# Two of sixteen hidden blocks of the first group changed from whole fp32 products to split fp32r products, with the instruction order rebuilt

## The chip, the cores and the metric

The kernel runs on one core of one Trainium2 chip. The metric is the device time of one execution in microseconds (us); the figure compared is the median of several runs. The core has five engines that matter here: PE (TensorE, matrix products; PEld is its weight load), DVE (VectorE), ACT (ScalarE), POOL (GpSimd) and SP (SyncE, which only issues DMAs here).

## The reference

Gated linear attention over 4 batches and 8 heads, 768 steps, head size 48, and then a feed-forward layer on its output:

```python
for t in range(S):
    state = alpha[:, :, t, :, None] * state + np.einsum('bhd,bhe->bhde', k[:, :, t], v[:, :, t])
    y[:, :, t] = np.einsum('bhd,bhde->bhe', q[:, :, t], state)
x = y.transpose(0, 2, 1, 3).reshape(3072, 384)
h = x @ w_in                          # w_in 384 x 2048
g = np.where(h >= 1, h, np.where(h <= -1, 0.0, (h + 1) ** 2 / 4))
return (g @ w_out).astype(np.float32) # w_out 2048 x 384
```

The two weight matrices come as float64 and are turned into fp32 on the chip.

## The kernel before

**Attention.** The 3072 tokens are 24 chunks of 128 (6 per batch, the batches in turn). For each chunk `prepare` loads gates, keys, queries and values (1.28 MB) and runs two scans and two products on DVE (L478 to L510); `begin_chunk` turns the keys (a PE transpose for chunks 0 to 6, later a DVE transpose and DMAs); the scores and the state update are short fp32 matmuls on PE (L589, L602). `follow` masks the scores: on DVE by a product with a 0/1 mask (L709, two halves u for each of two head parities r), or, for r = 1 of chunks 0 to 6 (`HELP`), by two ACT copies (L681) and one POOL `affine_select` (L691). Then the outputs of the chunk are computed (L769) and copied to x by `end_chunk`. From chunk 5 on (`MERGE`) the outputs of chunk j-1, the update and the scores of chunk j are one burst on PE; before, they are separate pieces.

**Feed-forward.** Three chunks are a group (8 groups of 384 tokens). A group has 16 blocks of 128 hidden units. `hidden` makes h for one block, then ACT and DVE make g (L918 twice, L928), and `second` adds g times its rows of w_out to three PSUM banks that stay open over the group. In group 0 (`WHOLE = 1`) both products are whole fp32 matmuls (L878, L960), on weights as decoded. In groups 1 to 7 both are split: weight and operand are each a sum of a rounded fp32r part and an fp32r rest, and three fp32r products (part by part, part by rest, rest by part) stand for one fp32 product (L887, L969). This needs a cast on ACT and a subtraction on DVE for g (L937, L938) and for x (L804, L809).

**Weights.** Each of 8 pairs of blocks has two tensors (in and out). A tensor is loaded as float64, decoded by ACT and DVE (L349 to L388, five instructions), and, for the split form, parted by `part_w` into a new buffer: an ACT cast (L394) and then, for pairs 0 to 4 (`BYSUM`), an ACT negation (L397) and an accumulating DMA issued by POOL (L402), or, for pairs 5 to 7, a DVE subtraction (L395). Decoded and parted tensors share one pool of `2 * NU + MORE` = 18 buffers of 6 KB per partition; 16 of them hold the decoded tensors, and a decoded one is free once it is parted and its blocks of group 0 are done.

**Order.** `Plan` gathers every instruction with a cost and a key (a due time, in units of one block) and orders all engines by a list scheduler written in the kernel: on each engine, of the instructions that can start soon, the one with the smallest key goes first. The constants at the top of the file and the table `OFF` shift keys. Where PE would be idle near the start, matmuls on zeros (`fill`, L1020) are put in. The order is fixed when the kernel is built; each engine runs its list in that order and waits on semaphores.

Of the kernel before, what the change touches and what calls it, by code (L numbers as in the profile page):

```python
# [27 lines left out]
WHOLE = 1  # L28
PLACED = (0, 1, 2, 5)
MORE = 2  # L30
NV = 3
WARM = 10
LAG = 4.0
FETCH = 9
LOAD = 12.0
DECODE = 3.5
PARTED = 4.0
PREPARE = 0.5
# [12 lines left out]
HELP = 7  # L51
BYSUM = 5
LATE = 14
TURN = 7
EARLY = 3.0
BYDMA = 24
NEAR = 0.2


OFF = {'b0': 4.6, 'b1': -0.3, 'b2': -25, 'b5': -25, 'b6': 3.7, 'b7': 3.5, 'di0': -6.0, 'di1': 2.6, 'di2': 2.7, 'di4': -0.2, 'di5': -0.8, 'di6': -0.8, 'di7': 2.3, 'do0': 5.0, 'do1': -1.1, 'do2': 0.1, 'do4': -0.1, 'do5': 0.3, 'do6': 0.5, 'fi0': -6.2, 'fi1': -10.5, 'fi2': 1.1, 'fi3': 2.0, 'fi4': 1.4, 'fi5': 0.2, 'fi6': -0.6, 'fi7': 17.6, 'fo0': -15.3, 'fo1': -6.3, 'fo2': 2.4, 'fo3': 1.9, 'fo4': 12.3, 'fo5': 7.6, 'fo6': -8.0, 'fo7': 1.1, 'l0': -6.5, 'l1': 0.1, 'l2': -6.9, 'l3': -2.8, 'l4': 3.7, 'l5': -12.4, 'l7': -0.8, 'l8': 0.3, 'p0': -0.3, 'p1': -0.4, 'p2': 0.2, 'p3': -20.7, 'p4': 1.6, 'p5': 1.3, 'p7': -1.3, 'p8': 1.5, 'q0': 0.1, 'q1': 5.5, 'q2': -22.8, 'q3': 15.7, 'q4': -13.5, 'q5': -8.8, 'q6': -14.1, 'q7': 14.6, 'q8': -14.2, 't1': 2.7, 't2': -24.0, 't3': 0.9, 't4': -1.7, 't5': -8.7, 't6': -8.6, 't8': -8.1, 'v0': 3.6, 'v1': 9.0, 'v2': -6.4, 'v3': 1.8, 'v4': 11.4, 'v5': -8.3, 'v6': -3.5, 'v7': 0.3, 'v8': 9.8, 'wi0': 0.3, 'wi2': -4.3, 'wi3': -19.9, 'wi4': -19.0, 'wi5': -0.7, 'wi6': 4.0, 'wi7': 10.0, 'wo0': -0.7, 'wo2': -6.1, 'wo3': 2.3, 'wo4': 1.4, 'wo5': -3.3, 'wo6': 2.7, 'wo7': 25, 'y1': 0.1, 'y2': 1.0, 'y3': -5.9, 'y4': -1.8, 'y5': -10.9}  # L60
off = lambda *k: OFF.get("".join(map(str, k)), 0.0)

# [179 lines left out]
def gated_attention_ffn(ctx: ExitStack, tc: tile.TileContext, q, k, v, alpha, w_in, w_out, by, out):  # L242
# [61 lines left out]
    with ExitStack() as main:  # L304
# [86 lines left out]
        def part_w(u, which, raw, parts, key):  # L391
            part = lambda a: parts().rearrange(PARTS[which])[:, a * n_w : (a + 1) * n_w]
            data = lambda: whole_w(raw())
            plan.op("ACT", 0.83, key, lambda: nc.scalar.copy(out=part(0), in_=data()), [raw], [parts])  # L394
            sub = lambda e: e.tensor_tensor(out=part(1), in0=data(), in1=part(0).bitcast(F32), op=ALU.subtract)  # L395
            if u < BYSUM:
                plan.op("ACT", 0.86, key, lambda: nc.scalar.mul(out=part(1), in_=part(0).bitcast(F32), mul=-1.0), [parts], [parts])  # L397
                plan.op(
                    "POOL",
                    1.0,  # L400
                    key,
                    lambda: nc.gpsimd.dma_start(out=part(1), in_=data(), accum_op=ALU.add),  # L402
                    [raw, parts],
                    [parts],
                    moved=P * n_w * 4,
                    land=0.8,
                    rate=Plan.SUM,
                )
                return
            plan.op("DVE", 0.95, key, lambda: sub(nc.vector), [raw, parts], [parts], port=True)  # L410
# [245 lines left out]
        def follow(j, key):  # L656
# [17 lines left out]
            for r, to in enumerate((Q, other)):  # L674
                for u in range(2):
                    if r and j < HELP:
                        plan.op(
                            "ACT",
                            0.39,
                            key,  # L680
                            lambda u=u: nc.scalar.copy(out=other()[0:HC, :, halves[u]], in_=ss(j, 1)[halves[u]]),  # L681
                            [meets[j][1]],
                            [other],
                            beside=True,
                        )
                        if u:
                            plan.op(
                                "POOL",
                                0.62,
                                key,  # L690
                                lambda: nc.gpsimd.affine_select(  # L691
                                    out=other()[0:HC].rearrange("p g (u t) -> p g u t", u=2),
                                    in_=other()[0:HC].rearrange("p g (u t) -> p g u t", u=2),
                                    compare_op=ALU.is_ge,
# [4 lines left out]
                                ),  # L699
                                [other],  # L700
                                [other],
                                port=True,
# [54 lines left out]
        whole_x = lambda n: xs[n]()[:, rest_n : rest_n + KT * groups[n] * CH].rearrange("p (k j t) -> p k j t", k=KT, j=groups[n])  # L757
        plan.op("POOL", 0.75, -98.0, lambda: nc.gpsimd.memset(rest_b(), 0.0), [], [xs[0]])

        def outputs(j, ps):  # L760
# [106 lines left out]
        def hidden(n, f, key):  # L867
# [3 lines left out]
            gf = buf("fw", "gf", [P, L], 3)  # L871
            whole = n < WHOLE

            def product():
                m = 0
                for kt in range(KT):
# [9 lines left out]
                    for w, a in ((0, 0), (0, 1), (1, 0)):  # L886
                        nc.tensor.matmul(  # L887
                            out=h(),
                            lhsT=win(f, w)[:, kt],
                            rhs=xs[n]()[:, 0 : groups[n], kt, a],  # L890
                            start=(m == 0),
# [4 lines left out]
            u = f // NW  # L896
            needs = [xs[n], *([*[("x", first[n] + c) for c in range(groups[n])], raws_w[u][0]] if whole else [("moved", n), wi[u]])]

# [50 lines left out]
        def second(seg, f, gh, key):  # L949
# [4 lines left out]

            whole = n < WHOLE

# [66 lines left out]
        for u in range(NU):  # L1023
            weights(u)
        at = 0

        for j in range(NCH):
# [217 lines left out]
```

## Time and profile before

| | |
|---|---|
| median of 3 runs | 501.81 us (501.47 to 501.83) |
| the profiled execution | 501.42 us, of which 499.7 us is the span from its first to its last instruction |
| PE busy | 491.5 us (98% of the span) |
| DVE busy | 347.3 us (69%) |
| ACT busy | 317.9 us (64%) |
| POOL busy | 30.5 us (6%) |
| granted TensorE clock, mean | 0.999 |

The busy times are unions over the span. The shares are averages over stages: DVE and ACT are much busier in the first 150 us than later. A matmul on PE overlaps the next one, so the sum of single durations is more than the busy time; the pace of a run of matmuls is read from the chain, where a piece stands with its own length.

### The profile page before, as it was taken

What the parts mean: (1) busy time and instruction counts of PE and PEld (TensorE: products, weight loads), DVE (VectorE), ACT (ScalarE), POOL (GpSimd) and SP (SyncE); (2) the same over time, 40 slices, a digit from 0 to 9 for tenths busy, and PEclk for the clock granted to TensorE, in tenths of its full rate; (3) what the DMA queues carried; (4) which work ended last, traced back from release to release, by engine and by line L of the source; (5) the groups of instructions that cost most, each with busy time, mean ns of one, the idle gap of its engine ahead of it and who ended that gap; (6) DMA issues with size and microseconds to landing.
All of it is one profiled execution on the core that took longest, in us unless ns stands there. A gap on an engine that the chain in (4) does not pass through costs nothing.

```text
span 499.7 us, 11372 instructions
## 1 busy us (share of the span) xinstructions
PE 491.5 (98%) x4586; PEld 446.5 (89%) x4586; DVE 347.3 (69%) x609; ACT 317.9 (64%) x603; POOL 30.5 (6%) x70
## 2 busy tenths in 40 slices
PE   8899999999999999999999999999999999999996
PEld 3665656699999999999999999999999999999995
DVE  6998999998997866865866857767755635343332
ACT  3799998998765565565665655665565655555551
POOL 4211102211000000000000000000000000000000
PEclk9999999999999999999999999999999999999999
DMA  8999916878552531542434513434313201001001
GB/s 315 394 387 387 330 23 142 208 201 181 181 159 65 187 102 49 150 137 82 110 95 118 174 47 124 130 100 139 115 35 89 70 1 25 1 7 42 0 1 51
DMA packets 43336, 64.42 MB, mean 129 GB/s; under 512 B 21392, under 2 KB 30736, under 8 KB 43280
## 3 DMA queue, kind: packets, MB, share of 16 engines
q1 hardware_dynamic: 41840, 59.71, 37.4%
q0 software_dynamic: 1440, 3.93, 4.2%
q8 instruction: 38, 0.62, 0.5%
q14 instruction: 18, 0.15, 0.1%
HBM read 48.56 MB, written 9.18 MB: 116 GB/s over the span
## 4 chain that ended last, share of the span: by engine, by line
PE 94%; DVE 3%; issue 1%; DMA 1%; POOL 0%; ACT 0%; DVEq 0%
PE ps L969 36%; PE ps L887 35%; PE ps L878 6%; PE ps L960 6%; PE ps L769 5%; PE ps L602 3%; PE ps L589 2%; DVE inv L485 1%; DVE pre L478 1%; DMA raw_a<-in_al 1%; PE ps L574 1%; DVE inv L493 0%; DVE Q L709 0%; DVE Q L510 0%; DVE state L653 0%
## 5 line engine op out<-in xcount | busy, mean ns | idle before, releaser
L969 PE MATMUL ps<-gh,wt 128*128 128x384 f32 x1008 | 197.1, 340 | 0.0
L887 PE MATMUL ps<-xs,wt 128*128 128x384 f32 x1008 | 193.6, 335 | 0.0
L969 PEld LDWEIGHTS ps<-gh,wt 128*128 128x128 f32 x1008 | 177.7, 188 | 1.3 <-issue 0.2
L887 PEld LDWEIGHTS ps<-xs,wt 128*128 128x128 f32 x1008 | 176.7, 188 | 0.7
L928 DVE SCALAR_TENSOR_TENSOR gf<-gf,ps 128x384 f32<-128x384 f32 x128 | 70.6, 552 | 94.0 <-ACT gf L918 92.5
L918 ACT ACTIVATE gf<-ps,half_b 128x384 f32<-128x384 f32 x128 | 74.4, 582 | 83.4 <-PE ps L887 80.5
L937 ACT CAST gh<-gf 128x384 fp32r<-128x384 f32 x112 | 57.4, 513 | 59.0 <-DVE gf L928 49.7
L938 DVE TENSOR_TENSOR gh<-gf,gh 128x384 fp32r<-128x384 f32 x112 | 62.0, 555 | 33.3 <-ACT gh L937 32.6
L918 ACT ACTIVATE gf<-gf 128x384 f32<-128x384 f32 x128 | 67.2, 525 | 4.0
L635 ACT COPY both<-state 48x192 f32<-48x192 f32 x88 | 30.8, 350 | 10.5 <-PE ps L602 9.1
L960 PE MATMUL ps<-gf,wt 128*128 128x384 f32 x96 | 33.0, 488 | 0.4 <-PE ps L878 0.4
L878 PE MATMUL ps<-xs,wt 128*128 128x384 f32 x96 | 32.7, 489 | 0.1
L478 DVE TENSOR_TENSOR_SCAN pre<-raw_a,fwd 128x516 f32<-128x516 f32 x24 | 29.5, 1228 | 3.0 <-DMA raw_a<-in_al 2.7
L485 DVE TENSOR_TENSOR_SCAN inv<-raw_a,bwd 128x516 f32<-128x516 f32 x24 | 30.1, 1254 | 2.1
L769 PEld LDWEIGHTS ps<-Q,both 128*64 128x64 f32 x368 | 23.2, 138 | 7.2 <-issue 5.6
L960 PEld LDWEIGHTS ps<-gf,wt 128*128 128x128 f32 x96 | 18.0, 190 | 12.4 <-PE ps L878 0.8
L878 PEld LDWEIGHTS ps<-xs,wt 128*128 128x128 f32 x96 | 17.8, 190 | 11.9 <-ACT wt L357 0.4
L769 PE MATMUL ps<-Q,both 128*64 128x64 f32 x368 | 26.6, 225 | 0.0
L769 PE MATMUL ps<-other,both 128*64 128x64 f32 x368 | 26.6, 225 | 0.0
L501 POOL COPY meet<-inv 128x4 f32<-128x4 f32 x24 | 9.8, 408 | 258.3 <-DVE inv L485 258.3
L769 PEld LDWEIGHTS ps<-other,both 128*64 128x64 f32 x368 | 23.2, 138 | 0.0
L709 DVE TENSOR_TENSOR Q<-ps,mask 64x256 f32<-64x256 f32 x48 | 20.3, 423 | 3.6 <-ACT other L672 1.8
(62 smaller groups left out, 370.1 us busy)
## 6 DMA issues: line engine op xcount, KB each, us to landing
raw_kq<-in_kq SPq DMA_DIRECT2D x24, 512.0 KB, 5.2
both<-in_vl SPq DMA_DIRECT2D x24, 512.0 KB, 4.6
raw_a<-in_al SPq DMA_DIRECT2D x24, 258.5 KB, 3.3
wt<-in_w_out SPq DMA_DIRECT2D x8, 768.0 KB, 9.4
wt<-in_w_in SPq DMA_DIRECT2D x8, 768.0 KB, 8.4
out<-ot SPq DMA_DIRECT2D x24, 192.0 KB, 3.1
turned<-w SPq DMA_DIRECT2D x17, 256.0 KB, 2.2
ks<-turned SPq DMA_DIRECT2D x68, 64.0 KB, 2.6
```

Source lines behind the costliest of these rows:

```text
L478: lambda: nc.vector.tensor_tensor_scan(flat(pre()), a[:, 0:n], flat(fwd), 0.0, ALU.mult, ALU.max),
L485: lambda: nc.vector.tensor_tensor_scan(flat(inv())[:, ::-1], a[:, 1 : n + 1][:, ::-1], flat(bwd)[:, ::-1], 0.0, ALU.mult, ALU.max),
L635: lambda r=r, to=to: nc.scalar.copy(out=to, in_=state[low[r], b]),
L769: nc.tensor.matmul(out=ps()[halves[r], to, halves[u]], lhsT=lhsT[:, u, r], rhs=x()[:, g, halves[u]], start=m + u == 0, stop=True, skip_gro ...
L878: nc.tensor.matmul(out=h(), lhsT=raw_in(f)[:, kt], rhs=whole_x(n)[:, kt].rearrange("p j t -> p (j t)"), start=kt == 0, stop=kt == KT - 1,)
L887: nc.tensor.matmul(out=h(), lhsT=win(f, w)[:, kt], rhs=xs[n]()[:, 0 : groups[n], kt, a], start=(m == 0), stop=(m == 3 * KT - 1),)
L918: lambda: nc.scalar.activation(out=gf(), in_=in_(), func=func, scale=scale, bias=bias),
L928: lambda: nc.vector.scalar_tensor_tensor(out=gf(), in0=gf(), scalar=1.0, in1=h(), op0=ALU.min, op1=ALU.max),
L937: plan.op("ACT", 0.08 + 0.41 * w, key + 0.4, lambda: nc.scalar.copy(out=gh()[:, 0], in_=gf()), [gf], [gh])
L938: sub = lambda e: e.tensor_tensor(out=gh()[:, 1], in0=gf(), in1=gh()[:, 0].bitcast(F32), op=ALU.subtract)
L960: nc.tensor.matmul(out=o_ps[seg][m](), lhsT=raw_out(f)[:, m * P : (m + 1) * P], rhs=gh(), start=f == f0, stop=f == f1 - 1,)
L969: nc.tensor.matmul(out=o_ps[seg][m](), lhsT=wout(f, w)[:, m * P : (m + 1) * P], rhs=gh()[:, a], start=(f == f0 and i == 0), stop=(f == f1 ...
```

## The change

The last two blocks (14 and 15, one pair) of group 0 are computed in split form (`PLAIN = 14`). For that, a new function `split_x` parts the x of group 0's three chunks into a new tile `xl` (9 KB per partition), pair 7 is parted in the time of group 0 instead of group 1, and g of these two blocks is parted too. To make room, the weight pool goes from 18 to 17 buffers (`MORE`) and the tile `gh` from 3 buffers to 2. For chunks 0 to 2 (`HELP0 = 3`) the masks of r = 0 go from DVE to ACT and POOL as well, and for r = 1 this is done for chunks 0 to 9 (`HELP = 10`) instead of 0 to 6. Bursts begin with chunk 4 instead of 5 (`MERGE`). `BYCAST` is 0, so its branch in `part_w` is never taken. All margins and most of `OFF` are new, so the order is another one.

```diff
-MORE = 2
+MORE = 1
+PLAIN = 14
+SPLIT = 3.5
+HELP0 = 3
+BYCAST = 0
-FETCH = 9
+FETCH = 10
-PARTED = 4.0
+PARTED = 5.0
-MARGIN0 = 18.0
-MARGIN1 = 8.0
+MARGIN0 = 9.0
+MARGIN1 = 6.0
-DECODE0 = 10.0
-AHEAD = 26
-FIRST = 3
+DECODE0 = 7.0
+AHEAD = 30
+FIRST = 4
-LATER = 8
-MERGE = 4
+LATER = 4.5
+MERGE = 3
-SOON = 5.5
-HELP = 7
+SOON = 8
+HELP = 10
-OFF = {'b0': 4.6, ...}
+OFF = {'b1': -0.2, ...}
...
-    step = [groups[n] / 3 * (1.2 if n < WHOLE else 1.0) for n in range(NG)]
+    step = [groups[n] / 3 * (1 + 0.2 * PLAIN / NF if n < WHOLE else 1.0) for n in range(NG)]
...
-            key = begin[WHOLE] + u * NW * step[WHOLE] - PARTED
+            n = 0 if (u + 1) * NW > PLAIN else WHOLE
+            key = begin[n] + u * NW * step[n] - PARTED
...
-                    if r and j < HELP:
+                    if j < (HELP0, HELP)[r]:
...
+        xl = buf("xs", "xl", [P, 2, KT, groups[0] * CH], 1, F32R)
+
+        def split_x(n):
+            key = begin[n] + PLAIN * step[n] - SPLIT
+            for c in range(groups[n]):
+                j = first[n] + c
+                to = lambda a, c=c: xl()[:, a].rearrange("p k (j t) -> p k j t", j=groups[n])[:, :, c]
+                o = plan.op(
+                    "ACT", 0.5, key + off("x", j), lambda c=c, to=to: nc.scalar.copy(out=to(0), in_=whole_x(n)[:, :, c]),
+                    [xs[n], ("x", j)], [xl], beside=c > 0,
+                )
+                plan.op(
+                    "DVE", 0.55, key + off("x", j),
+                    lambda c=c, to=to: nc.vector.tensor_tensor(
+                        out=to(1), in0=whole_x(n)[:, :, c], in1=to(0).bitcast(F32), op=ALU.subtract
+                    ),
+                    [xs[n], ("x", j)], [xl], beside=True, after=[o], port=True,
+                )
...
-            whole = n < WHOLE
+            whole = n < WHOLE and f < PLAIN
+            split = lambda kt, a: xl()[:, a, kt] if n < WHOLE else xs[n]()[:, 0 : groups[n], kt, a]
...
-            gh = buf("fw", "gh", [P, 2, L], 3, F32R)
+            gh = buf("fw", "gh", [P, 2, L], 2, F32R)
...
+        for u in range(NU):
+            parts_of(u)
...
-                if at == WHOLE:
-                    for u in range(NU):
-                        parts_of(u)
+                if at < WHOLE and PLAIN < NF:
+                    split_x(at)
```

## Rows read from the trace of the kernel before

**Rows 1.** Waits of PE: engine, line, waited-for engine and line: us, times, longest.

```profile
PE ps L574 <- DVE inv L493: 1.6, 2, 0.9
PE ps L960 <- PE ps L878: 0.4, 1, 0.4
```

**Rows 2.** Chain that ended last, in order of time: start us, us, what.

```profile
28.53 4.12 PE ps L878 x12
33.09 2.10 PE ps L960 x6
...
71.07 3.87 PE ps L878 x12
74.94 3.87 PE ps L960 x12
...
96.31 2.78 PE ps L960 x8
99.09 3.14 PE ps L887 x18
...
106.64 1.58 PE ps L969 x9
...
166.58 1.59 PE ps L969 x9
...
172.87 1.58 PE ps L969 x9
```

**Rows 3.** Timeline of DVE: start us, us, engine line op tiles [idle before].

```profile
10.48 1.63 DVE L485 TENSOR_TENSOR_SCAN inv<-raw_a,bwd 128x516 f32<-128x516 f32 x1
...
15.55 1.23 DVE L485 TENSOR_TENSOR_SCAN inv<-raw_a,bwd 128x516 f32<-128x516 f32 x1
16.82 0.86 DVE L709 TENSOR_TENSOR Q<-ps,mask 64x256 f32<-64x256 f32 x2
...
27.47 0.96 DVE L388 CUSTOM_DVE_ANT_0 wt<-wt,w 128x1536 uint16<-128x1536 uint16 x1
...
32.23 0.55 DVE L928 SCALAR_TENSOR_TENSOR gf<-gf,ps 128x384 f32<-128x384 f32 x1
...
93.94 0.96 DVE L388 CUSTOM_DVE_ANT_0 wt<-wt,w 128x1536 uint16<-128x1536 uint16 x1
...
169.72 0.53 DVE L938 TENSOR_TENSOR gh<-gf,gh 128x384 fp32r<-128x384 f32 x1
```

**Rows 4.** Timeline of POOL, chunk 0's mask.

```profile
10.37 0.66 POOL L691 TENSOR_SCALAR_AFFINE_SELECT other<-other 64x512 f32<-64x512 f32 x1
```

**Rows 5.** Groups by line and shape: busy us, mean ns of one | idle before.

```profile
L938 DVE TENSOR_TENSOR gh<-gf,gh 128x384 fp32r<-128x384 f32 x112 | 62.0, 555 | 33.3 <-ACT gh L937 32.6
L937 ACT CAST gh<-gf 128x384 fp32r<-128x384 f32 x112 | 57.4, 513 | 59.0 <-DVE gf L928 49.7 <-DVE bwd L482 6.8 <-PE ps L969 2.1
L395 DVE TENSOR_TENSOR wt<-wt 128x768 fp32r<-128x768 f32 x6 | 5.7, 946 | 0.0
L681 ACT COPY other<-ps 64x256 f32<-64x256 f32 x14 | 5.1, 368 | 0.6 <-PE ps L602 0.5
```

**Rows 6.** Busy time by stage: us, PE, PEld, DVE, ACT, POOL, PEclk, DMA, GB/s.

```profile
25.00:50.00 25.00, 24.39 (x208) 15.18 (x207) 23.10 (x33) 22.96 (x36) 2.99 (x5) 1.00 1.01 387
50.00:75.00 25.00, 25.00 (x142) 15.05 (x141) 23.64 (x35) 23.10 (x39) 3.01 (x4) 1.00 0.55 177
75.00:98.00 23.00, 23.00 (x270) 15.07 (x269) 21.02 (x35) 20.72 (x37) 5.32 (x9) 1.00 0.73 169
```

**Rows 7.** Timeline of ACT: a parting cast that waited, and its negation.

```profile
84.15 0.83 ACT L394 CAST wt<-wt 128x768 fp32r<-128x768 f32 x1 [1.05 <-DMA wt<-wt]
85.01 0.84 ACT L397 ACTIVATE wt<-wt 128x768 fp32r<-128x768 f32 x1
```

**Rows 8.** Lines L394 and L402: ns min/median/max, first and last start; time to landing.

```profile
L394 ACT CAST wt<-wt x16: 807/829/838, 42.2 to 134.7; 128x768 fp32r<-128x768 f32 x16
...
DMA to landing us min/median/max: 3.9/6.3/9.8
```

More of the change, by code (lines that the diff above doesn't have):

```diff
@@ L29 @@
 PLACED = (0, 1, 2, 5)
-MORE = 2
+MORE = 1
 NV = 3
+PLAIN = 14
+SPLIT = 3.5
+HELP0 = 3
+BYCAST = 0
 WARM = 10
 LAG = 4.0
-FETCH = 9
-LOAD = 12.0
+FETCH = 10
+LOAD = 12
 DECODE = 3.5
-PARTED = 4.0
-PREPARE = 0.5
+PARTED = 5.0
+PREPARE = 1.0
 MARGIN = 9.0
-MARGIN0 = 18.0
-MARGIN1 = 8.0
+MARGIN0 = 9.0
+MARGIN1 = 6.0
 FETCH0 = 16
-DECODE0 = 10.0
-AHEAD = 26
-FIRST = 3
+DECODE0 = 7.0
+AHEAD = 30
+FIRST = 4
 ROOM = 6
-LATER = 8
-MERGE = 4
+LATER = 4.5
+MERGE = 3
 WARMTH = 40
-SOON = 5.5
-HELP = 7
+SOON = 8
@@ L393, in part_w @@
             data = lambda: whole_w(raw())
-            plan.op("ACT", 0.83, key, lambda: nc.scalar.copy(out=part(0), in_=data()), [raw], [parts])
+            hi = (parts, "hi")
+            if u >= NU - BYCAST:
+                plan.op(
+                    "POOL",
+                    1.0,
+                    key,
+                    lambda: nc.gpsimd.dma_start(out=part(0), in_=data()),
+                    [raw],
+                    [parts, hi],
+                    moved=P * n_w * 4,
+                    land=0.8,
+                    rate=Plan.SUM,
+                )
+                plan.op("ACT", 0.86, key, lambda: nc.scalar.mul(out=part(1), in_=data(), mul=-1.0), [raw], [parts], beside=True)
+                plan.op(
+                    "POOL",
+                    1.0,
+                    key,
+                    lambda: nc.gpsimd.dma_start(out=part(1), in_=data(), accum_op=ALU.add),
+                    [raw, parts],
+                    [parts],
+                    moved=P * n_w * 4,
+                    land=0.8,
+                    rate=Plan.SUM,
+                )
+                return
+            plan.op("ACT", 0.83, key, lambda: nc.scalar.copy(out=part(0), in_=data()), [raw], [parts, hi])
             sub = lambda e: e.tensor_tensor(out=part(1), in0=data(), in1=part(0).bitcast(F32), op=ALU.subtract)
@@ L680, in follow @@
                             key,
[L681 to L684, printed above, removed]
+                            lambda r=r, u=u, to=to: nc.scalar.copy(out=to()[halves[1 - r], :, halves[u]], in_=ss(j, r)[halves[u]]),
+                            [meets[j][r], other],
+                            [to],
+                            beside=r + u > 0,
                         )
+                        masks.append(o)
                         if u:
@@ L690, in follow @@
                                 key,
-                                lambda: nc.gpsimd.affine_select(
-                                    out=other()[0:HC].rearrange("p g (u t) -> p g u t", u=2),
-                                    in_=other()[0:HC].rearrange("p g (u t) -> p g u t", u=2),
+                                lambda r=r, to=to: nc.gpsimd.affine_select(
+                                    out=to()[halves[1 - r]].rearrange("p g (u t) -> p g u t", u=2),
+                                    in_=to()[halves[1 - r]].rearrange("p g (u t) -> p g u t", u=2),
                                     compare_op=ALU.is_ge,
@@ L699, in follow @@
                                 ),
-                                [other],
-                                [other],
+                                [to],
+                                [to],
                                 port=True,
@@ L889, in product @@
                             lhsT=win(f, w)[:, kt],
-                            rhs=xs[n]()[:, 0 : groups[n], kt, a],
+                            rhs=split(kt, a),
                             start=(m == 0),
@@ L896, in hidden @@
             u = f // NW
-            needs = [xs[n], *([*[("x", first[n] + c) for c in range(groups[n])], raws_w[u][0]] if whole else [("moved", n), wi[u]])]
+            if whole:
+                needs = [xs[n], *[("x", first[n] + c) for c in range(groups[n])], raws_w[u][0]]
+            else:
+                needs = [*([xl] if n < WHOLE else [xs[n], ("moved", n)]), wi[u]]
             firsts[:] = [
@@ L953, in second @@
                 o_ps[seg] = [bank("ps_o", KT, [P, L]) for _ in range(KT)]
-            whole = n < WHOLE
+            whole = n < WHOLE and f < PLAIN
             def product(ms):
```

11 lines of the change are left out of this document (7 added, 4 removed).

## The prediction

> **What bounds the kernel now.** I read the waits of PE first. All waits of PE in the whole execution are a few, short, and lie at the start: the largest is 1.6 us on the products that `prepare` makes on DVE, and the latest is 0.4 us before the first second-layer block [rows 1]. From 33 us to the end of the last block PE never waits. So past 33 us the time can fall only by less work on PE, and it can rise by any stall that comes in; before 28.53 us, when the first hidden block starts [rows 2], it is what holds that start.
>
> Next, the chain in order of time, for the pace of PE. Two hidden blocks in whole form are one piece of 3.87 us, so one is 1.935 us, and two second-layer blocks took the same; two hidden blocks in split form are 3.14 us, so one is 1.57 us, and a split second-layer block is 1.58 us [rows 2]. The first piece after attention matmuls is some 0.2 us longer (4.12 against 3.87) [rows 2].
>
> Then the timeline of DVE, for the start. It works almost without a gap from 3.8 us on, through the preparation of chunks 0 to 3, their masks and the decoding of the first weight tensor, whose last instruction ends at 28.43 us, 0.1 us before the first hidden block [rows 2, 3]. So DVE sets the start. The 0.4 us before the first second-layer block is DVE's too: it makes g at 32.23 to 32.78 us and PE goes on at 33.09 us [rows 2, 3].
>
> Last, busy time by stage, for the cover under group 0. Of 73 us from 25 to 98 us, DVE is idle 1.90 + 1.36 + 1.98 = 5.24 us, and ACT 2.04 + 1.90 + 2.28 = 6.22 us [rows 6]. Both engines nearly fill group 0, although PE does not wait for them.
>
> **The change part by part.**
>
> *Two blocks in split form.* Two hidden blocks fall from 3.87 us to 3.14 us and two second-layer blocks from 3.87 us to 3.16 us: 0.73 + 0.71 = 1.44 us less on PE, which is the bound there. Both forms are measured at this size and the granted clock is 1.00 in these stages [rows 6], so this term I take as it stands.
>
> *Masks off DVE at the start (`HELP0`).* For each of chunks 0, 1 and 2, two mask products on DVE, 0.86 us together [rows 3], become two ACT copies of 0.37 us [rows 5] and one POOL select of 0.66 us [rows 4]. That is 3 x 0.86 = 2.6 us off the engine that sets the start. It does not come free: a select on POOL at 10.37 us lies over the scan that starts at 10.48 us, which took 1.63 us where its like took 1.23 us [rows 3, 4], so a select can cost DVE 0.40 us. Taking half of that for each, since a select may also meet an instruction that it leaves alone, the gain is 3 x (0.86 - 0.20) = 2.0 us; the bounds are 0 (if the longer way over ACT and POOL holds chunk 2's x until the old time) and 2.6 us. I take 2.0, because DVE's list and not the latency of a chunk ends just before the first block.
>
> The Trainium skill (SBUF — State Buffer, section Who interferes with whom) says that a DVE instruction with two SBUF inputs and a GpSimd instruction that reads SBUF share a port, and that the loser is blocked for the whole of the other. The 0.40 us that the scan lost agrees in kind, with less than the select's whole 0.66 us. By that rule in full the gain at the start would be 3 x (0.86 - 0.66) = 0.6 us, and the forecast 1.4 us later; it speaks against this part of the change.
>
> *The first wait of the second layer.* Chunk 3 becomes due later than the first block (its margin falls by 2 and its shift rises), so the g of the first block can come ahead of chunk 3's masks on DVE: up to 0.4 us [rows 1]. Bounds 0 and 0.4; I take 0.4.
>
> *Bursts from chunk 4 on.* The separate outputs of chunk 3 join a burst; one change between attention and blocks goes, 0.2 us [rows 2].
>
> *More work on DVE and ACT in group 0.* Parting x: three casts and three subtractions of the size of those of g, 3 x 0.51 us on ACT and 3 x 0.56 us on DVE. Parting g of two blocks: 2 x 0.51 and 2 x 0.56 us. Pair 7 parted there instead of later: 2 x 0.83 on ACT and 2 x 0.95 on DVE [rows 5, 8]. Sum: DVE 1.67 + 1.11 + 1.89 = 4.67 us, ACT 4.2 us. What hides it is the idle time of the two engines, 5.24 and 6.22 us. But group 0 also becomes shorter on PE by 1.44 + 0.2 us; so DVE would need 4.67 + 1.64 = 6.3 us and has 5.24. The lack of 1.1 us, and the 0.4 us of the item before, which only moves PE ahead of the same DVE work, comes back as a wait at the end of group 0 if DVE can't be filled better. That end is tight already: the last decoding of a weight tensor starts at 93.94 us and ends at 94.90 us, and the second-layer blocks that follow in the chain start at 96.31 us [rows 2, 3]; now a parting of some 1.8 us must fit between. Bounds 0 (the work of chunks 6 and 7 is put off) and 1.5 us. Behind a late second-layer block 14 stand block 15 and the outputs of group 0 on PE, and then group 1. I take the middle, 0.75 us.
>
> *Masks of chunks 7 to 9 (`HELP`).* 6 x 0.43 us leave DVE after group 0 and 6 x 0.37 us come to ACT. PE never waits there, so this alone gives nothing; it is cover.
>
> *Two buffers of `gh` instead of three.* In the steady state the cast of a block can start once the second-layer block two before it is done: that one ends at 168.17 us, the subtraction starts at 169.72 us and ends at 170.25 us, and the block that reads it starts at 172.87 us [rows 2, 3]. That leaves 2.6 us, so two buffers cost nothing; without that cover the cost would be what a late subtraction is late by.
>
> *One weight buffer less.* See the first rival; in the forecast it costs nothing, with the early start of the casts as cover.
>
> Sum against the profiled execution: 501.42 - 1.44 - 2.0 - 0.4 - 0.2 + 0.75 = 498.1 us. That execution lies 0.4 us under the median of 501.81 us; the same change from the median gives 498.5 us, which I predict. Everything at its better bound is 1.44 + 2.6 + 0.4 + 0.2 = 4.6 us from the profiled run, so 496.8 us; with the start's gain at 0 and 1.5 us lost at the end of group 0 it is 501.42 - 1.44 - 0.2 - 0.4 + 1.5 = 500.9 us.
>
> **The rivals.**
>
> *One spare weight buffer starves group 1 (slower).* A parted tensor needs a free buffer and gives one back only when its source has been read and its blocks in group 0 are done. With 18 buffers two partings can be under way, with 17 one. The trace shows that buffers are already what partings wait for: a cast waited 1.05 us for an accumulating DMA and began as it landed [rows 7]. With two buffers the 16 casts ran from 42.2 to 134.7 us, one per 6.2 us [rows 8]. One parting by the DMA takes 0.83 + 0.84 us and 6.3 us to land [rows 7, 8], 8.0 us when nothing else is in the way; ten of these and six with DVE at some 2.5 us (0.83 + 0.95 and the gaps) are 95 us one after another. The last must be there when block 13 of group 1 runs: 99.09 us and 13 blocks of 3.15 us, 140 us, plus bursts. From 42 us that is 98 us, just enough; but a tensor parted early, before its blocks are done, holds the buffer idle until then. If that happens for 20 us, as a cast of pair 4 at some 45 us that waits for blocks 8 and 9 at 65 us would do, the lack is about 17 us at the end of the chain, part of which the faster landings (3.9 us, 2.4 us under the median, ten times) take back. I price it at 5 to 8 us: 503.5 to 506.5 us. It decides from the point at which the mean time per parting passes 98 / 16 = 6.1 us. For it: the wait in [rows 7]. Against it: PE had no wait at all for a parted tensor, and the order sees the count of buffers.
>
> *DVE eats the gain (no change).* If DVE can't be filled beyond its present share in group 0 (67.76 of 73 us, 93% [rows 6]), the start's gain is given back: 4.67 us more work at 93% need 5.0 us, less the 2.6 us that went before, and 0.4 us for selects: PE would reach group 1 some 2.8 us late against its new place, which leaves 501.42 - 4.04 + 2.8 = 500.2 us, and with another 1 us in group 1, where the selects for chunks 7 to 9 fall, 501.2 us. For it: the shares of DVE. Against it: work of later chunks in group 0 can be put off.
>
> *The start does not move.* If chunk 2's latency over ACT and POOL holds the first block at 28.5 us, only 1.44 + 0.2 + 0.4 us are left: 499.4 us from the profiled run. It lies within the forecast's range.
>
> **How the numbers follow.** About 0.2% (1 us) is what a measurement here can tell from no change. Forecast with its bounds, 496.5 to 500.8 us: 0.62. No change by the DVE rival, or the gain and a small stall cancelling, 500.8 to 502.8 us: 0.15. Slower by the buffer rival, from 502.8 us on: 0.23. For 8 in 10 the range goes from 496.3 us over the no-change case to 503.3 us. Its likeliest part is 496.5 to 500.8 us.
>
> **What the profile would show.** The first hidden block near 26 us instead of 28.53; 12 fewer whole matmul rows each at the lines of the whole products, and 18 more split ones; DVE at 97% or more from 25 to 95 us. If the waits of PE show the parted weights or the ACT cast and the accumulating DMA before split hidden blocks between 95 and 145 us, the buffer rival is right. If they show DVE's g or parting of pair 7 at 85 to 95 us, the DVE rival is. The prediction is wrong too if the new order puts more of chunk 3's preparation ahead of the first block, or if PE waits for `gh` after a burst.

## The result, and the profile after

The changed kernel takes 507.4 us (median of four runs, 506.1 to 508.1), the kernel before 501.6 us beside it: a ratio of 1.0114, with a 95% interval of 1.0102 to 1.0126. It is slower by 5.8 us, and the time lies 4.1 us above the upper end (503.3 us) of the range that the prediction gave for 8 in 10.

The profiled execution, with 508.1 us the slowest of the four, has a span of 506.4 us, which is 6.7 us more than the 499.7 us of before. Four points that both traces have in common say where the 6.7 us lie. The second point is the place where TensorE (PE) has done all blocks of group 0 and the hidden products of four blocks of group 1, and begins the first second-layer block of group 1. The work up to it is the same in both kernels but for the four block halves that the change splits.

| stretch | before, us | after, us | difference |
| --- | --- | --- | --- |
| start of the span to the first hidden block | 28.53 | 28.04 | -0.49 |
| from there to the first second-layer block of group 1 | 78.11 | 83.61 | +5.50 |
| from there to the last copy of an output tile | 388.60 | 388.59 | -0.01 |
| from there to the end of the span | 4.46 | 6.16 | +1.70 |

The first two points before are in [rows 2] (28.53 and 106.64 us), and those after in the chain below. The last copies, before and after, end their chains:

```profile
495.24 0.56 DVE ot L330
```

```profile
500.24 0.56 DVE ot L334
```

Nothing is lost in groups 1 to 7. What is lost lies in group 0 and behind the last copy. The waits of PE and ScalarE (ACT) name the place in group 0 (columns as in [rows 1]):

```profile
ACT wt L424 <- DMA wt<-wt: 7.0, 3, 4.2
...
PE ps L1024 <- ACT wt L424: 1.8, 1, 1.8
PE ps L939 <- ACT wt L424: 1.2, 1, 1.2
```

Neither of these waits of PE was there before [rows 1]. L424 is the cast that makes the rounded part of a weight tensor, L394 in [rows 7]; L425 is the subtraction for its rest; L939 and L1024 are the split hidden and second-layer products, L930 and L1015 the whole ones. (In the experiments some line numbers are shifted.) PE waits for the cast, and the cast waits for a DMA. The chain, in order of time, shows which one:

```profile
28.04 4.14 PE ps L930 x12
...
81.12 5.93 DMA wt<-wt
...
87.12 0.83 ACT wt L424
...
89.18 0.73 ACT wt L424
...
91.08 7.72 DMA wt<-wt
...
98.88 0.84 ACT wt L424
...
99.74 0.97 DVE wt L425
...
100.75 1.97 PE ps L1024 x7
102.72 4.22 PE ps L939 x18
106.94 1.58 PE ps L1024 x9
108.53 3.12 PE ps L939 x18
111.65 1.59 PE ps L1024 x9
```

It is read from below. The seven products at 100.75 us wait for the rest of the last pair's output weights, made at 99.74 us from a cast at 98.88 us. That cast waited for an accumulating DMA that was on its way from 91.08 us for 7.72 us. The DMA belongs to another tensor, parted from 89.18 us on. It brings nothing that the cast reads: it still reads the decoded tensor whose buffer becomes the one spare buffer, into which the cast is to write. That cast stood for 4.2 us, the longest wait at L424. The first cast of the last pair, at 87.12 us, had waited in the same way for the DMA of 81.12 us. The timeline of PE shows how long PE stood for both, and for what VectorE (DVE) makes behind them (L524 is a product of `prepare`, L605 the transpose of the keys that reads it):

```profile
88.01 0.62 PE L939 MATMUL ps<-xl,wt 128*128 128x384 f32 x2 [1.24 <-ACT wt L424]
89.00 1.49 PE L939 MATMUL ps<-xl,wt 128*128 128x384 f32 x7 [0.38 <-DVE wt L425]
90.96 0.63 PE L605 MATMUL ps<-ident,inv 128*128 128x128 f32 x4 [0.47 <-DVE inv L524]
...
99.76 0.62 PE L1024 MATMUL ps<-gh,wt 128*128 128x384 f32 x2 [1.83 <-ACT wt L424]
100.75 1.97 PE L1024 MATMUL ps<-gh,wt 128*128 128x384 f32 x7 [0.38 <-DVE wt L425]
```

The five waits of PE are 1.24 + 0.38 + 0.47 + 1.83 + 0.38 = 4.30 us. There is a price on top. In stages of four us (columns as in [rows 6]):

```profile
84.00:88.00 4.00, 2.77 (x9) 1.33 (x7) 3.08 (x7) 2.35 (x7) 1.78 (x2) 1.00 0.69 181
88.00:92.00 4.00, 3.14 (x17) 2.53 (x18) 3.87 (x6) 3.91 (x7) 0.93 (x2) 1.00 0.32 84
...
96.00:100.00 4.00, 2.17 (x7) 1.03 (x7) 0.32 (x2) 1.10 (x3) 0.00 (x0) 1.00 0.59 182
100.00:104.00 4.00, 3.62 (x14) 3.31 (x14) 3.84 (x7) 3.90 (x9) 0.66 (x1) 0.70 0.01 4
104.00:108.00 4.00, 4.00 (x22) 4.00 (x21) 3.94 (x8) 2.94 (x6) 1.56 (x2) 0.88 0.40 64
```

PE was busy for 2.17 of the four us from 96 us on, and behind that the granted clock is 0.70 and then 0.88 in the mean, between its two levels of 1.2 GHz (0.5) and 2.4 GHz; 0.30 x 4 + 0.12 x 4 = 1.7 us of full pace are missing. The pieces say the same: eighteen hidden products took 4.22 us where the next eighteen took 3.12 us, and the seven products at 100.75 us took 1.97 us where the seven at 89.00 us, at a clock of 1.00, took 1.49 us: 1.10 + 0.48 = 1.6 us. So the two waits at 99.76 and 100.75 us, 2.2 us together, cost another 1.6 us by the clock. From 84 to 92 us PE also stood, for 1.23 and 0.86 us, and there the clock stayed at 1.00.

Each wait at L939 and L1024 has a small price besides: the two and the seven products behind a wait took 0.62 and 1.49 us at 1.00, where two and seven ninths of 1.58 us are 0.35 and 1.23 us. At 0.27 us for each of the four it is 1.1 us. The sum, 4.3 + 1.6 + 1.1 = 7.0 us, is what is to be explained: without loss the stretch would be 78.11 us less the 1.44 us of PE's work that the split form saves, and it is 83.61 us, 6.9 us more.

The start moved by 0.49 us, not by 2.0 us. The masks that left DVE became selects on GpSimd (POOL), and the timelines of POOL and DVE show what they took and what they did to their neighbours:

```profile
10.37 0.66 POOL L723 TENSOR_SCALAR_AFFINE_SELECT Q<-Q 64x512 f32<-64x512 f32 x1 [0.33 <-ACT Q L712]
11.13 0.95 POOL L723 TENSOR_SCALAR_AFFINE_SELECT other<-other 64x512 f32<-64x512 f32 x1
...
20.64 1.70 POOL L723 TENSOR_SCALAR_AFFINE_SELECT Q<-Q 64x512 f32<-64x512 f32 x1 [0.24 <-POOL xs L760]
```

```profile
10.57 1.00 DVE L524 TENSOR_TENSOR inv<-inv,raw_kq 128x512 f32<-128x512 f32 x1
11.49 1.13 DVE L541 TENSOR_TENSOR Q<-pre,raw_kq 128x512 f32<-128x512 f32 x1
...
16.16 0.69 DVE L524 TENSOR_TENSOR inv<-inv,raw_kq 128x512 f32<-128x512 f32 x1
16.77 1.15 DVE L541 TENSOR_TENSOR Q<-pre,raw_kq 128x512 f32<-128x512 f32 x1
...
20.64 1.23 DVE L509 TENSOR_TENSOR_SCAN pre<-raw_a,fwd 128x516 f32<-128x516 f32 x1
```

Beside a select, DVE's products took 1.00 to 1.15 us, and 0.69 us without one. The selects were stretched too, from 0.66 us [rows 4] to 1.70 us beside a scan of DVE, which kept its 1.23 us. In these rows the one that begins second is longer by what the other has left, less 0.14 to 0.19 us. The product at 10.57 us begins with 0.46 us of the first select to come, and takes 0.31 us longer; the select at 11.13 us, with 0.44 us of that product to come, 0.29 us longer; the select at 20.64 us, with the whole scan to come, 1.04 us longer. So either side loses in turn.

At the end, the last copy is where it was within its stretch, but the transfers behind it are slower. The last DMA issues of SyncE (SP) in the timeline, before and after:

```profile
494.77 1.39 SPq L1008 DMA_DIRECT2D out<-ot  x3
```

```profile
499.77 2.37 SPq L1063 DMA_DIRECT2D out<-ot  x3
```

The three issues took 2.37 us for 1.39 us, and landed in 2.9 us (median) for 1.9 us. Why is open (see the sum below).

### The profile page after: what moved, and what is told of

It reads as the page before. It is cut to its first block, busy times and chain, and to the rows that moved or that the text cites. A ratio compares the mean times of both kernels' runs of the same rounds, so it can differ in the third digit from the quotient of the medians.

```text
span 506.4 us, 11534 instructions
## 1 busy us (share of the span) xinstructions
PE 492.1 (97%) x4594; PEld 449.3 (89%) x4594; DVE 346.3 (68%) x602; ACT 323.1 (64%) x620; POOL 39.1 (8%) x76
## 4 chain that ended last, share of the span: by engine, by line
PE 88%; DMA 4%; ACT 3%; DVE 2%; issue 2%; POOL 0%; DVEq 0%; ACTq 0%; POOLq 0%
PE ps L1024 36%; PE ps L939 35%; PE ps L820 4%; PE ps L930 4%; PE ps L1015 3%; DMA wt<-wt 3%; PE ps L633 2%; PE ps L620 2%; ACT wt L424 1%; DMA raw_a<-in_al 1%; PE ps L1075 1%; DVE inv L516 0%; DVE pre L509 0%; DVE Q L541 0%; ACT both L666 0%
## 5 line engine op out<-in xcount | busy, mean ns | idle before, releaser
L1024 PE MATMUL ps<-gh,wt 128*128 128x384 f32 x1026 | 201.4, 340 | 2.2 <-ACT wt L424 1.8
L939 PE MATMUL ps<-xs,wt 128*128 128x384 f32 x1008 | 194.1, 336 | 0.0
L1024 PEld LDWEIGHTS ps<-gh,wt 128*128 128x128 f32 x1026 | 181.1, 188 | 4.4 <-ACT wt L424 2.4
L939 PEld LDWEIGHTS ps<-xs,wt 128*128 128x128 f32 x1008 | 177.9, 189 | 0.1
L992 ACT CAST gh<-gf 128x384 fp32r<-128x384 f32 x114 | 58.8, 516 | 44.5 <-PE ps L1024 43.3
L993 DVE TENSOR_TENSOR gh<-gf,gh 128x384 fp32r<-128x384 f32 x114 | 63.1, 554 | 30.0 <-ACT gh L992 28.8
L666 ACT COPY both<-state 48x192 f32<-48x192 f32 x88 | 30.8, 349 | 10.1 <-PE ps L633 9.0
L1015 PE MATMUL ps<-gf,wt 128*128 128x384 f32 x84 | 29.3, 491 | 0.0
L930 PE MATMUL ps<-xs,wt 128*128 128x384 f32 x84 | 28.5, 487 | 0.0
L930 PEld LDWEIGHTS ps<-xs,wt 128*128 128x128 f32 x84 | 15.8, 190 | 10.9 <-DVE wt L392 0.3
L1015 PEld LDWEIGHTS ps<-gf,wt 128*128 128x128 f32 x84 | 15.6, 190 | 10.4 <-PE ps L930 0.4
L741 DVE TENSOR_TENSOR Q<-ps,mask 64x256 f32<-64x256 f32 x42 | 17.8, 423 | 3.1 <-ACT other L703 2.3
```

Of the source, the lines that this page charges most:

```text
L666: lambda r=r, to=to: nc.scalar.copy(out=to, in_=state[low[r], b]),
L930: nc.tensor.matmul(out=h(), lhsT=raw_in(f)[:, kt], rhs=whole_x(n)[:, kt].rearrange("p j t -> p (j t)"), start=kt == 0, stop=kt == KT - 1,)
L939: nc.tensor.matmul(out=h(), lhsT=win(f, w)[:, kt], rhs=split(kt, a), start=(m == 0), stop=(m == 3 * KT - 1),)
L993: sub = lambda e: e.tensor_tensor(out=gh()[:, 1], in0=gf(), in1=gh()[:, 0].bitcast(F32), op=ALU.subtract)
L1015: nc.tensor.matmul(out=o_ps[seg][m](), lhsT=raw_out(f)[:, m * P : (m + 1) * P], rhs=gh(), start=f == f0, stop=f == f1 - 1,)
L1024: nc.tensor.matmul(out=o_ps[seg][m](), lhsT=wout(f, w)[:, m * P : (m + 1) * P], rhs=gh()[:, a], start=(f == f0 and i == 0), stop=(f == f1 ...
```

## The experiments

Theory: the one spare weight buffer, held from the cast of a tensor until its accumulating DMA has landed, keeps the last pair from being parted in time, and PE stands for it in group 0. First rival: it is the splitting itself, too much work for ACT and DVE in group 0. Second rival: it is the rebuilt order, and the buffers don't matter.

### One spare buffer alone, and the change without its split blocks

The first kernel is the one before with one number changed. The second is the changed one with all sixteen blocks of group 0 whole again. The order of each is rebuilt with it.

```diff
-MORE = 2
+MORE = 1
```

```diff
-PLAIN = 14
+PLAIN = 16
```

> The kernel before with one edit: 17 weight buffers instead of 18 (the order is rebuilt from it). Buffer theory (one spare buffer lets only one parting run, each holds it until its accumulating DMA has landed, 4 to 8 us): casts wait for landings several times over, PE waits for parted tensors in group 0's end or group 1, 3 to 10 us slower than before, 504.5 to 511.5 us. Rival (pair 7 of the changed kernel comes too late because its decoding and parting find no room on DVE and ACT in group 0, whatever the buffers): here pair 7 is parted in group 1's time, so no wait, 501.6 us within 1 us.

> The changed kernel with all 16 blocks of group 0 whole again (no parting of x or of pair 7 in group 0), one spare buffer and the rest of the change kept. Buffer theory: the casts still wait for landings, and PE waits in group 1, where pairs 0 to 6 come late; 503 to 510 us. Rival (pair 7's work in group 0): the waits at 86 to 101 us are gone and none takes their place, 1.4 us more PE work, 0.5 us from the start: 501 us within 1 us.

Measured: 506.8 us for the first, a ratio of 1.012 [1.010, 1.0145]; 502.2 us for the second, 1.0011 [0.9999, 1.0022]. The waits of the first, and a stage of it:

```profile
ACT wt L394 <- DMA wt<-wt: 8.7, 5, 3.0
...
PE ps L969 <- DMA wt<-wt: 2.6, 1, 2.6
```

```profile
125.00:150.00 25.00, 22.36 (x211) 21.66 (x210) 21.86 (x39) 18.05 (x36) 2.32 (x4) 1.00 0.59 151
```

One spare buffer costs the kernel before 5.3 us, without any split block in group 0; there PE falls short in group 1 (busy for 22.36 of 25 us from 125 us on), where the prediction's rival looked for it. Behind this wait of 2.6 us the clock stayed at 1.00. The second kernel has the same one spare buffer, and no wait of PE behind the start: its casts still wait for DMAs, four times and 3.2 us in all, but early enough for PE. In time it lies between what the rival expected (500 to 502 us) and the theory (503 us or more), nearer to the rival. So one spare buffer is enough or not by what is due when, and the changed kernel's loss needs the last pair's early due time as well. An order rebuilt from the changed kernel's due times, in the second kernel, doesn't make it.

### The accumulating DMAs made short

The changed kernel with its order untouched, but an accumulating DMA moves 48 of the 768 columns, so that the rests of pairs 0 to 4 stay incomplete.

```diff
-nc.gpsimd.dma_start(out=part(1), in_=data(), accum_op=ALU.add)
+nc.gpsimd.dma_start(out=part(1)[:, 0:48], in_=data()[:, 0:48], accum_op=ALU.add)
```

> The changed kernel, its order untouched; the ten accumulating DMAs move 48 of 768 columns each, so the rest of the fp32r rests of pairs 0 to 4 is left out. Buffer theory (the one spare buffer is held until an accumulating DMA of 4 to 8 us has landed, and pair 7 queues behind it): the casts no longer wait for landings; the waits of PE before blocks 14 and 15 shrink from 4.3 us to under 1.5 us, the clock stays at its upper level, 501 to 503.5 us. Rival (DVE and ACT have no room for pair 7's decoding and parting before blocks 14 and 15): the waits stay, 505 to 508 us.

Measured: 502.9 us, 1.0026 [1.0015, 1.0038]. The casts wait for a DMA once, for 1.3 us; behind the start PE waits 1.1 us for DVE's L425 and 0.5 us for L524, and the clock is 1.00 throughout. That gives back 4.5 us. It leaves open whether the short hold or the lighter traffic did it.

### A second spare buffer under the same order

The same order again, all transfers whole, and one weight buffer more. The room comes from x: its rest is worked out into a scratch that nobody reads, and the third product of blocks 14 and 15 reads the rounded part instead; two output tiles of three lie in the scratch of the decode.

```diff
-wts = ctx.enter_context(tc.tile_pool(name="wts", bufs=2 * NU + MORE))
+wts = ctx.enter_context(tc.tile_pool(name="wts", bufs=2 * NU + 2))
-xl = buf("xs", "xl", [P, 2, KT, groups[0] * CH], 1, F32R)
+xl = buf("xs", "xl", [P, KT + 1, groups[0] * CH], 1, F32R)
-split = lambda kt, a: xl()[:, a, kt] if n < WHOLE else ...
+split = lambda kt, a: xl()[:, kt] if n < WHOLE else ...
```

> The changed kernel with its instructions in the order that it has, and one weight buffer more, so that two are spare. The room for it comes from two places: the rest of x of blocks 14 and 15 is still worked out, but into 384 columns of which each of the three writes covers the last, and the third product of these two blocks reads the rounded part instead of the rest; two of the three output tiles lie in a buffer of the ring of the decode's scratch. Theory (the loss in group 0 is the one spare buffer, held until an accumulating transfer has landed, whatever that transfer moves): no wait of TensorE on a cast of the last pair, granted clock 0.97 or more in 84 to 108, the stretch from the first block to the first block of group 1 within 1 us of 78.1, and 502.3 to 503.5 us, as with the small sums (502.86). Rival (with the small sums it was the lighter traffic that helped, not the shorter hold): the casts wait for transfers as in the changed kernel and the time stays at 505.5 to 507.5 us.

Measured: 502.8 us, 1.0024 [1.0014, 1.0033]. Its stages, then its chain (L1034 is L1024 here):

```profile
84.00:88.00 4.00, 3.14 (x11) 1.70 (x9) 3.82 (x7) 3.93 (x9) 1.78 (x2) 1.00 0.72 187
88.00:92.00 4.00, 3.34 (x19) 3.05 (x20) 3.96 (x7) 3.43 (x6) 1.14 (x2) 1.00 0.56 135
...
96.00:100.00 4.00, 4.00 (x22) 3.59 (x21) 3.81 (x9) 3.87 (x9) 0.66 (x1) 1.00 0.24 94
```

```profile
28.06 4.14 PE ps L930 x12
...
106.55 1.58 PE ps L1034 x9
```

From the first block to the first second-layer block of group 1 are 106.55 - 28.06 = 78.49 us, for 83.61 us: 5.1 us come back (4.6 us between the medians, 507.4 and 502.8 us), with the traffic as it was. The wait at 99 us is gone, and the loss of clock with it. The theory holds and the rival of the lighter traffic falls. What stays is a wait of 1.04 us for DVE's L425 and one of 0.47 us for L524, 1.51 us together, in the stages from 84 to 92 us. They are not the buffer's: they are DVE's.

### Two spare buffers under rebuilt orders

Here the room for the second buffer comes from keeping the parts of x in the buffers of g (`gh`, three again), and the order is rebuilt with it.

```diff
-MORE = 1
+MORE = 2
-xl = buf("xs", "xl", [P, 2, KT, groups[0] * CH], 1, F32R)
+xl = [buf("fw", "gh", [P, 2, groups[0] * CH], 3, F32R) for _ in range(KT)]
```

> The changed kernel with two spare buffers again (18) and three of gh; the parted x of group 0 lies in the three tiles of gh for as long as blocks 14 and 15 need it. Buffer theory: casts no longer wait for landings, the 4 us of waits before parted weights shrink to under 1.5 us and the clock doesn't drop: 500.5 to 503 us. Rival (pair 7's work in group 0): the waits before blocks 14 and 15 stay, 505 to 508 us.

Measured: 505.3 us, 1.0079 [1.0060, 1.0097]: the time of the rival, and by another wait than either theory had. The casts wait for no DMA any more. PE stands for 2.1 us before a second-layer block in whole form (L1012):

```profile
87.88 3.73 PE ps L1012 x6
```

```profile
88.00:92.00 4.00, 4.00 (x18) 1.88 (x20) 3.63 (x6) 3.94 (x6) 2.27 (x4) 0.57 0.50 95
```

Again a low clock follows, 0.57, and six products take 3.73 us, where twelve in [rows 2] take 3.87 us. What ended the wait is not shown for certain. The profile names a copy of the state on ACT (L666), but the last step of a decoding (L392) ended 0.1 us before PE went on, as one did before the first block in the kernel before, and the block may read that tensor. To see whether DVE's subtractions of x make that wait, the next kernel does them on 16 of 384 columns (and reads the rounded part in the third product of blocks 14 and 15), in the same order:

> The kernel with two spare buffers and pair 7 split in group 0 (505.3 us), its order untouched; the three DVE subtractions for x of group 0 work on 16 of 384 columns, and the third product of blocks 14 and 15 reads the rounded part in place of the rest. DVE theory (with the buffer given back, DVE's list is what is late: PE waited 2.1 us at 85.8 us for the end of a decoding): 1.4 us less DVE work ahead of it leaves a wait under 1 us, and the clock does not fall after it: 501.5 to 503.5 us. Rival (another chain, such as a DMA or ACT, holds PE there): the wait stays at 2 us, 505 us.

Measured: 505.1 us, 1.0072 [1.0051, 1.0094], with the wait of 2.1 us still there. The theory that DVE's subtractions make it falls. Then three kernels with other due times (numbers only, all in the changed kernel's code): the changed one with two spares, the same with sixteen whole blocks, and one with the whole blocks, two spares and bursts of the kernel before. The numbers also say for how many chunks masks are made by selects: `HELP` is 11, 12 and 9, and `HELP0` 3, 3 and 2, so that the third is not wholly the work of the kernel before.

> The changed kernel with two spare weight buffers (the rounded part and rest of x lie in three tiles of the gate's ring, which has three buffers again), as in the run before with two spares, and with other due times for the steps of preparation, the decodes and the partings, so that the order is another one. Theory (what the change cost in group 0 is the held weight buffer and, with the buffer given back, the place of the last pair's decode in the order; the splitting itself fits beside TensorE): no wait of TensorE above 1 us between 80 and 105 us, granted clock 0.95 or more in 85 to 105, 501.0 to 502.5 us. Rival (two more split blocks and their partings in the time of group 0 are more work than ScalarE and VectorE have room for there, whatever the order): a wait of 1 us or more stays before the second layer of the last block pairs, and the time stays at 504 to 506 us, as with the two spares before (505.3).

> The changed kernel's code with all sixteen blocks of group 0 whole, two spare weight buffers, three buffers for the gate, and other due times. What is left of the change is the order at the start. Theory: without pair 7 in group 0 and with the buffer back, nothing of the loss is left: 501.0 to 502.2 us, no casts that wait on a DMA for more than 2 us. Rival (what the change lost beyond the buffer sits in the rebuilt start): 503 us or more.

> The kernel before with other due times alone (same buffers, same work, no block of group 0 split): the yardstick for the other two. Theory: the start is what an order can still win, by the 0.5 to 2 us that the first block can come earlier, and the rest of the span is TensorE's: 500.0 to 501.8 us. Rival (any rebuilt order loses on the chip, since DMA landings and the shared port are not in the order's costs): 502.5 us or more, as the rebuilt order of the kernel before with help for the first chunks (506.6).

Measured: 505.3 us, 1.0072 [1.0026, 1.0117], for the first, with spans of single executions from 499.7 to 507.1 us; 503.7 us, 1.0042 [1.0029, 1.0055], for the second; 502.2 us, 1.0011 [1.0000, 1.0022], for the third. In time the rival has the first two, and the third lies between its theory and its rival. But the stages of the first show what the question was about:

```profile
85.00:90.00 5.00, 5.00 (x123) 3.85 (x121) 4.66 (x7) 4.85 (x8) 0.00 (x0) 1.00 0.79 234
90.00:95.00 5.00, 5.00 (x29) 3.35 (x19) 4.89 (x10) 4.36 (x10) 0.66 (x1) 1.00 0.23 89
```

PE has no wait there: the split blocks, the parting of x and that of the last pair do fit beside ACT and DVE in this order. The same matmuls as in the second row of the table run from 30.7 us to some 106.8 us there (the last nine of them begin at about 105.3 us and take 1.56 us), which is 76.1 us, 2.0 us less than before. The order lost it elsewhere: the first block starts 2.2 us late, behind a wait of 2.2 us for L524 and a granted clock of 0.72 and 0.86 from 8 to 16 us, and PE stands later for the landing of a transposed k (L633 updates the state):

```profile
117.03 0.62 PE L633 MATMUL ps<-both,ks 64*64 64x48 f32 x26 [1.95 <-DMA ks<-turned]
```

So that the split blocks fit at no price elsewhere is not shown. The second kernel lost time otherwise: PE waited 1.8 us for transfers of the x of a later group, and its granted clock is 0.81 and 0.76 from 24 to 32 us. None of these orders beats the kernel before, and neither does the third, which is nearest to it.

### The start

The selects alone: the changed kernel's code with the numbers of the kernel before and whole blocks (`PLAIN = 16`), its order rebuilt. Against the kernel before that is:

```diff
+HELP0 = 3
```

> The kernel before with one edit: r = 0 masks of chunks 0 to 2 go to ACT and POOL (HELP0 = 3), with the order rebuilt. Port theory (DVE and POOL instructions hold each other up, so what the masks give DVE is lost again in instructions stretched from 0.7 to 1.1 us and selects from 0.66 to 1.5 us): first hidden block at 27.5 to 28.5 us. Rival (DVE is relieved by the whole 2.0 us, and something else of the new order held the start back): first hidden block at 26 to 26.8 us.

Measured: 506.6 us, 1.0101 [1.0084, 1.0118]. It tells nothing about the port: in the rebuilt order a load of weights lands 9.67 us after 19.22 us, and the first block waits for it until 31.4 us. So the next one leaves the order of the changed kernel untouched and lets the six early selects work on two elements (the masks of chunks 0 to 2 are left out):

> The changed kernel, its order untouched; the six POOL selects of chunks 0 to 2 work on two elements per partition, so the masks of these chunks are left out. Port theory (POOL selects and DVE instructions hold each other up in the first 28 us): the DVE instructions that took 1.0 to 1.15 us fall to 0.55 to 0.7 us, the selects vanish from the path, and the first hidden block starts at 26 to 27 us instead of 28.04. Rival (the start is set by something else, such as the loads): it stays within 0.4 us of 28. Either way the later waits stay, so the time falls by no more than the start does: 505 to 507.5 us.

Measured: 505.9 us, 1.0096 [1.0079, 1.0113]; the first block starts at 26.90 us, 1.1 us earlier, and the products of DVE are at their own length (its timeline):

```profile
16.29 0.68 DVE L541 TENSOR_TENSOR Q<-pre,raw_kq 128x512 f32<-128x512 f32 x1
```

The waits for the weight buffer are there as before, the longest of PE now 1.1 us; in the profiled execution, with 504.1 us the fastest of its four, the clock stayed at 1.00 behind them. Last, both edits together, the second buffer under the same order and the small selects:

> The kernel of the run beside it, and also the six early selects of GpSimd on two elements (so the masks of chunks 0 to 2 are left out). Theory (the two terms, the held buffer and the port shared by GpSimd and VectorE at the start, stand apart and add up): first block at about 26.9 us, no wait of TensorE behind it, 1.0 to 1.6 us under the run beside it: 501.0 to 502.3 us, at or a little under the kernel before. Rival (what comes earlier at the start is lost again at the next landing, whether of a weight or of a turned k): a wait of TensorE of 0.8 us or more between 30 and 110 us, and within 0.5 us of the run beside it.

Measured: 502.0 us, 1.0013 [1.0004, 1.0022], 0.85 us under the run beside it, just short of what was expected. No wait of 0.8 us for a landing of a weight or a k came in; the wait of 1.1 us for L425 is there as in the run beside it. But the start gave back less than in the run with the small selects alone. Its chain, and that of the run with the small selects alone, say why:

```profile
10.75 8.73 DMA both<-in_vl
...
27.88 4.02 PE ps L938 x12
```

```profile
10.80 7.69 DMA both<-in_vl
...
26.90 4.05 PE ps L938 x12
```

With the selects small, the start hangs on the landing of a load of v, which took 8.73 us in one execution and 7.69 us in the other, and the first block comes 1.0 us later in the one than in the other. With whole selects this load can set the start too. In the run with the short accumulating DMAs it took 8.76 us, and the chain leads from it to the first block:

```profile
28.31 4.14 PE ps L930 x12
```

So the selects are to be priced at like landings. At 7.7 us, which the load took in the changed kernel as well, small selects start the first block at 26.90 us for 28.04 us, 1.1 us earlier; at 8.7 us at 27.88 us for 28.31 us, 0.4 us earlier. Each of these is one execution.

## Why the prediction was wrong, point by point

**The step that failed** is "One weight buffer less": "in the forecast it costs nothing, with the early start of the casts as cover". It cost 5.1 us of the stretch (83.61 against 78.49 us with the buffer back), 2.8 us as waits, 1.6 us as lost clock and 0.8 us as the small price behind each of three more waits. The rival "One spare weight buffer starves group 1" had the mechanism, at 0.23 and at 503.5 to 506.5 us (measured 507.4 us), but looked for it over the 98 us up to 140 us, as a mean time per parting. The casts did end later, and PE met none of that in group 1 (columns as in [rows 8]):

```profile
L424 ACT CAST wt<-wt x16: 815/830/839, 47.4 to 145.1; 128x768 fp32r<-128x768 f32 x16
...
DMA to landing us min/median/max: 4.0/4.7/7.7
```

The last cast began at 145.1 us for 134.7 us [rows 8]. What counted was the earliest due time: the same change that took the buffer moved two partings to 87 and 99 us, where two landings of 5.9 and 7.7 us fell in front of them. A landing of that size was in view (3.9 to 9.8 us [rows 8]), and so was a cast that had waited for one [rows 7].

**Masks off DVE at the start.** 2.0 us forecast, 0.49 us measured. The mechanism is the one the prediction names, its size was off. The forecast took 0.20 us per select, 0.6 us in all; DVE lost 0.31, 0.44 and 0.46 us in the three products shown (0.69 us without a select) and as much in a step of the decode, 1.7 us in all, where 0.40 us had been lost before [rows 3]. The selects were held up besides, the last ones beside DVE's scans, and the chain to the first block leads over one of them (1.48 us at 22.40 us). With the six of them cut to two elements 1.1 or 0.4 us more came, by the landing of the load of v, which the prediction did not have in view. By a select's whole 0.66 us the prediction had worked out 0.6 us, near the 0.49 us; that is partly luck, since the losses were not three whole selects.

The rule behind that figure is in the Trainium skill (SBUF — State Buffer, section Who interferes with whom): whoever of the two starts first holds the shared port for its whole instruction, and the other is blocked. The trace agrees with it, less 0.14 to 0.19 us each time: the loser waits for what the other has left.

**The first wait of the second layer.** 0.4 us forecast, nothing measured: the first hidden block ends at 32.18 us and the second layer goes on at 32.61 us, 0.43 us as before [rows 2].

**Two blocks in split form.** The 1.44 us are there. The stretch with the buffer back is 78.11 - 1.44 + 1.51 us of waits = 78.18 us by this sum, 78.45 us with the 0.27 us behind the wait for L425, and 78.49 us as measured; in the order without a wait it is some 76.1 us, which also lacks the first wait of 0.43 us.

**More work on DVE and ACT in group 0.** 0.75 us forecast, within 0 and 1.5 us; 1.51 us measured with the buffer back, all for DVE, at the upper bound. So the rival "DVE eats the gain" was right in part. An order without this wait exists, though it lost time elsewhere.

**Two buffers of gh.** Nothing, as forecast: no wait of PE for g behind a burst. **Bursts** and the selects for chunks 7 to 9 were not tried by themselves.

**The sum.** Against the 498.1 us worked out for the profiled execution, its 508.1 us are 10.0 us more: 5.1 us for the buffer, 1.5 at the start, 0.8 for DVE's waits, 0.4 for the first wait, 0.5 for bursts and rest, 1.7 behind the last copy. The last term stood in no step. Its cause is open: from the last copy to the end it is 4.35 and 4.46 us in the two kernels with the old code and 4.6 to 6.5 us in the twelve with the new; two kernels with the same order (those with two spares, with and without the small x) have 4.6 and 5.5 us, so it isn't the order alone. It was not tried by itself. It is also what separates the run with the second buffer from the kernel before: there the last copy begins at about 495.2 us in both.

## What to carry to other kernels

When a change takes away a buffer, don't ask whether the buffers suffice in the mean: list the tensors by their due times after the change, and see whether between the two earliest there is room for one hold, from the first write to the landing of the last transfer that reads or adds to it. A change that spends room and moves a due time forward in one go is worth taking apart: here the same split blocks under the same order with the buffer kept took 5.1 us less, and the one spare buffer without the split blocks cost next to nothing in one order (502.2 us) and 5.3 us in another. A wait of PE of about two us is to be priced with the slower stretch that can follow it, and work moved from DVE to POOL with what both lose side by side.

## What the runs showed of the hardware that was not expected

A wait of PE of 1.8 + 0.4 us cost 1.6 us more by a granted clock of 0.70 and 0.88 behind it, and one of 2.1 us brought 0.57. But one of 2.6 us (one spare buffer alone) and one of 0.5 + 1.95 us (two spares in another order) left the clock at 1.00, and so did 1.23 and 0.86 us in neighbouring stages: in these runs the length of a wait alone does not say whether the clock falls. A select of 0.66 us took up to 1.70 us beside DVE, and products of 0.69 us took up to 1.15 us beside selects; in the pairs read, the one that began second was longer by what the other had left, less 0.14 to 0.19 us. And where it set the start, the landing of one load of 512 KB, 7.69 or 8.73 us in two executions of the same order, moved the first block by that difference.
